# Masks at the end of a score step, another order of the attention's steps, and earlier first weights

## The chip, the core and the metric

The kernel runs on one core of a Trainium2 chip. The metric is the device time of the kernel in microseconds (us). The engines are named as in the profile: PE (matrix engine, with PEld for its weight loads), DVE (VectorE), ACT (ScalarE), POOL (GpSimd) and SP (SyncE, which here issues most DMAs).

## The reference

Three layers follow each other: attention with a block-causal mask, a mixture of experts with noisy top-2 gating, and a second one with top-1 gating and a bias per modality.

```python
# 4 batches, 8 heads, 576 positions, 64 per head; blocks of 64
scores = scale * np.matmul(q, k.transpose(0, 1, 3, 2))
mask = block_i >= block_j
scores = np.where(mask, scores, -1000000000.0)
attn = np.exp(scores - np.max(scores, axis=-1, keepdims=True))
attn = attn / (np.sum(attn, axis=-1, keepdims=True) + 1e-09)
x = np.matmul(attn, v)                       # -> 2304 rows of 512
# first layer: 8 experts, the best 2 of each row by noisy logits
noisy_logits = x @ w_gate + np.log1p(np.exp(x @ w_noise)) * noise
out[mask] += top2_w[mask, k, None] * (np.maximum(x[mask] @ w1[e], 0.0) @ w2[e])
# second layer: 8 experts, the best 1
logits = x @ w_gate + modality_bias[modality_id]
out[mask] = gate_w[mask, None] * (np.maximum(x[mask] @ w1[e], 0.0) @ w2[e])
```

## The kernel before

The kernel works in float32 accuracy by splitting values into a high part (type fp32r) and a low part, the remainder, and multiplying in three passes: high x high, high x low, low x high.

The attention goes by 16 pairs of heads (4 batches x 4 pairs), in the first 325 us of the profile. Each pair is cut into some sixty named steps. TQ, TK and T4 transpose the loaded q, k and the tail of both on PE; QH, KH, A4 (ACT) and QL, KL, D4 (DVE) make the high and low parts. S4, S6, S0 and S8 are the score steps: S4 is block row 2 (384 columns), S6 block row 3 (512 columns), S0 the rows 0 and 1 together (256 columns each), S8 the tail of 64 rows of both heads. In S4, S6 and S0 the two heads of the pair sit in the two halves of PE's rows. A score step writes two of three banks ("ps" in the profile). M steps (DVE, "nm") take maxima, E steps (ACT, "p") exponentials with sums. The B steps and BT transpose the exponentials on PE into three banks that TQ, TK, T4 and the X steps use as well ("pt"); H (ACT, "PTh") and L (DVE, "PTl") copy them out in high and low parts. VX, V0 and V1 (PE, "pa", one bank) multiply by v, CX, C0, C1 (ACT, "oT") copy that out, X0 and X1 (PE, "pt<-IW,oT") turn it back and multiply by the gates, XC0 and XC1 (ACT, "xu") copy that out, and R and R2 make the reciprocals of the sums.

The mask is added by PE as a further product in each score step: two bfloat16 matmuls per block row (one per head) add a large negative number to the 64 columns that must not count. Before, they stand behind the first of the three passes.

The order on PE, ACT and DVE is the order in which the program is written, and a small planner writes it: it keeps a clock per engine from functions of cost (`pe_cost`, `act_cost`, `dve_cost`), and among the steps whose operands are there it takes, within 0.15 us of the earliest, the one with the smallest due time. The due time of step n of pair p is p x 13.5 (the first number of `SCHED`) plus the offset of n in the table `SCHED`. POOL and SP get their order from the framework. Two other kinds of work are put between: work at fixed planner times (`at`: constants, zero fills, the first weights), and the routing of the first layer (`route`, on DVE above all, with a few matmuls), which starts when pairs 7, 11 and 15 are done and runs beside the following pairs.

`consts2` and `consts3` load and prepare what the second gate needs; `consts3` has four transposes of "wg" and one small matmul of "bias" on PE and copies on ACT. The first weights of the first expert come in four pieces of 512 KB ("xs<-in_moe_w_dram"); for each, `stage.fetch` issues the DMA and `stage.split` makes the high part on ACT ("wh<-xs") and the low part on DVE in two instructions ("wl<-xs"). They are called in the loop over NQ = 4 at planner times 110, 124, ... (fetch) and 11 later (split).

After the last pair the expert stage follows: for each expert 128-row tiles of gathered rows, two matrix products with the split weights, scatter-adds of the result. There PE works almost without a break.

Of the kernel before, what the change touches and what calls it, by code (L numbers as in the profile page):

```python
# [7 lines left out]
F32 = mybir.dt.float32  # L8
F32R = mybir.dt.float32r
BF16 = mybir.dt.bfloat16  # L10
# [5 lines left out]
DRAM = bass.MemoryType.DRAM  # L16
ET = mybir.EngineType

SCHED = (13.500, {
# [6 lines left out]
})  # L26


def moe_kernel(tc, q, k, v, w_gate, w_noise, noise, w1, w2, mod_id, w_gate2, mod_bias, m2w1, m2w2, out):
# [27 lines left out]
    clk = {"pe": 0.0, "dve": 0.0, "act": 0.0, "pool": 0.0, "base": 0.0}  # L57
# [14 lines left out]
    def cols_of(t):  # L72
        n = 1
        for x in t.shape[1:]:
            n *= x
        return n
# [7 lines left out]
    def pe_cost(name, o, i, kw):  # L84
        n = cols_of(o)
        dt = i.dtype
        if name == "transpose":
            return n * .00084
        if i.shape[0] == 64:
            return n * .00021 + .04  # L90
        return 2 * max(cols_of(i) * .00084, n * .00084) if dt == F32 else n * .000417 + .0145 * (clk["base"] is None)

    def act_cost(name, o, i, kw):
# [6 lines left out]

    gps = Timed(nc.gpsimd, "pool", pool_cost)
    vec, ten, act = Timed(nc.vector, "dve", dve_cost), Timed(nc.tensor, "pe", pe_cost), Timed(nc.scalar, "act", act_cost)

    with ExitStack() as top:
        cst = top.enter_context(tc.tile_pool(name="cst", bufs=1))
        dram = top.enter_context(tc.tile_pool(name="dram", bufs=1, space=DRAM))
        X1 = dram.tile([NT + CAP, DM], F32, name="X1")
# [37 lines left out]
        base = cst.tile([128, E], F32, name="base")  # L145
# [232 lines left out]
        def at(t, f):  # L378
            heapq.heappush(heap, (t, len(seen), f))
            seen.append(0)  # L380
# [264 lines left out]
        stage = Stage([j00, j10] + firsts + seconds)  # L645
# [144 lines left out]
        with ExitStack() as ph:  # L790
# [14 lines left out]
            masks = [cst.tile([128, n], BF16, name="mask%d" % n) for n in (128, 64)]  # L805
# [12 lines left out]
            def consts0():  # L818
                vec.tensor_scalar(IW[:, :, 0:D], bc(jp[:, None, 0:D], [128, H, D]), -64.0, None, op0=OP.is_equal)
                vec.tensor_tensor(IW[:, :, 0:D], IW[:, :, 0:D], bc(ident[:, None, 0:D], [128, H, D]), op=OP.add)  # L820
                for a in range(2):
                    for i, w in enumerate((w_gate, w_noise)):
                        nc.sync.dma_start(IW[64 * a:64 * a + 64, :, D + E * i:D + E * i + E], w.rearrange("(h d) e -> d h e", d=D))
                for t in RR:
                    nc.gpsimd.memset(t[64:128, :, 4:5], 0.0)
                for t in XU:
                    nc.gpsimd.memset(t[64:128, :, 4], 0.0)
# [32 lines left out]
            def pair(p):  # L860
# [3 lines left out]
                st = {}  # L864
# [3 lines left out]
                f = {}  # L868
# [23 lines left out]
                def khi(src, s0, n):  # L892
                    act.activation(st["kh"][:, s0:s0 + n], src, AF.Copy)

                def klo(src, s0, n):
                    vec.tensor_sub(st["kl"][:, s0:s0 + n], src, st["kh"][:, s0:s0 + n].bitcast(F32))
# [16 lines left out]
                def D4():  # L913
                    for x in halves:
# [4 lines left out]
                         TK=TK, KH=lambda: khi(st["tk"], 0, 512), KL=lambda: klo(st["tk"], 0, 512), T4=T4, A4=A4, D4=D4)  # L919
# [8 lines left out]
                def mx(o, i):  # L928
                    vec.reduce_max(nm(i), o, axis=AX, negate=True)

                def ex(o, c, i, j):
                    act.activation(P[i][:, c:c + o.shape[-1]], o, AF.Exp, bias=nm(i), scale=1.0, accum_out=st["ss"][:, j:j + 1])

                def some(name, js):

                    def tile_of(h, n):
                        return st["s", js[0], h][:, 0 if n == js[0] else 256:][:, 0:128 * (n + 1)]

                    def S_():
                        for h in range(2):  # L940
                            st["s", js[0], h] = ps_s.tile([128, 512], F32, name="ps")
                        for n in js:
                            kn = max(256, 128 * (n + 1))
                            for m, (Q, K) in enumerate(((qh, "kh"), (qh, "kl"), (ql, "kh"))):
                                for h in range(2):
                                    d = slice(64 * h, 64 * h + 64)
                                    o = st["s", js[0], h][:, 0 if n == js[0] else 256:][:, 0:kn]
                                    ten.matmul(o, Q[d, 128 * n:128 * n + 128], st[K][d, 0:kn], start=(m == 0), stop=(m == 2))
                                if m == 0:

                                    for h in range(2):
                                        d = slice(64 * h, 64 * h + 64)
                                        ten.matmul(tile_of(h, n)[:, 128 * n + 64:], masks[0][d], masks[1][d], start=False, stop=False)
                    f["S" + name] = S_
                    for h in range(2):
                        f["M%s%s" % (name, "ab"[h])] = lambda h=h: [mx(tile_of(h, n), 2 * n + h) for n in js]
                        f["E%s%s" % (name, "ab"[h])] = lambda h=h: [ex(tile_of(h, n), 0, 2 * n + h, 2 * n + h) for n in js]
# [50 lines left out]
                for h in range(2):  # L1008
# [7 lines left out]
                       lambda T, o=o, m=m: T[:, :, o:o + m + 1:m].rearrange("p h c s -> p c h s")) for i, (o, m) in enumerate(((0, 9), (16, 5)))])  # L1016

                def BT():
# [7 lines left out]
                         LT=lambda: vec.tensor_sub(end[64:128], bt(slice(64, 128)), end[64:128].bitcast(F32)))  # L1026
# [180 lines left out]

            TT, OFF = SCHED[0], dict(SCHED[1])
            OFF.update(N8=OFF["M8"] + .1, R2=OFF.pop("R"))
# [80 lines left out]
            def earliest(e, p, n):  # L1290
                t = clk[e] if p > 2 or n not in arrive else max(clk[e], arrive[n] + 5.5 * p)
                for d, k in before[n]:
                    if p >= k:
                        if (p - k, d) not in fin:
                            return None
                        t = max(t, fin[p - k, d] + (0 if d[0] in "FG" else lag[engine(d)]))
                if n[0] in bank and e == "pe":
                    b = bank[n[0]][0]
                    m = 2 if n[0] == "S" else 1
                    for r in held[b][-nbank[b]:][:max(0, len(held[b][-nbank[b]:]) + m - nbank[b])]:  # L1300
                        if r not in fin:
                            return None
                        t = max(t, fin[r] + .1)
                return t
# [5 lines left out]
            emit(0, "VS", 0)  # L1310
            emit(1, "VS", 0)
            consts0()
            for t, f in ((14, consts1), (90, consts2), (110, consts3)):
                at(t, f)
            fills = [(X1, NTT, 2), (X1, NTT + 2, 3)] + [(X2, t, 2) for t in range(0, NTT + NP + 1, 2)]
            for i, a in enumerate(fills):
                at(60 + 10 * i, lambda a=a: blank(*a))
            for i in range(NQ):
                at(110 + 14 * i, lambda: stage.fetch(1))
                at(110 + 14 * i + 11, lambda: stage.split(vec))  # L1320
            while any(todo.values()) or len(aside) > 1 or "early" not in flags:
                best = None
                for e, l in todo.items():
                    c = []
                    for i, (due, p, n) in enumerate(l[:60]):
                        t = earliest(e, p, n)
                        if t is not None:
                            c.append((t, due, i))
                    if c:
                        m = min(c)[0]  # L1330
                        t, _, i = min((x for x in c if x[0] <= m + eps), key=lambda x: x[1])
# [6 lines left out]
                if aside:  # L1338
                    t = max(aside[0][0], clk["dve"])
                    if best is None or t <= best[0] and (t <= dve_next or t > aside[0][0] + patience):  # L1340
                        best = (t, None, 0)
                t, e, i = best
# [3 lines left out]
                if e:  # L1346
                    _, p, n = todo[e].pop(i)
# [6 lines left out]
                else:  # L1354
                    clk["base"] = t
                    d = next(aside[0][1], None)
# [204 lines left out]
        with tc.For_i(0, nc.values_load(more[0:1, 0:1], min_val=0, max_val=1), 1), tc.tile_pool(name="r1", bufs=1) as r1:  # L1561
# [12 lines left out]
            with tc.For_i(0, nc.values_load(eo[0:1, NG2:], min_val=0, max_val=NG2), 1):  # L1574
# [3 lines left out]
                for i in range(B):  # L1578
                    n = slice(10 * i, 10 * i + 10)
# [20 lines left out]
                h = [hs[f][0].bitcast(F32) for f in range(NF // 128)]  # L1600
# [30 lines left out]
            with tc.For_i(0, nc.values_load(er[0:1, NG2:], min_val=0, max_val=NG2), 1):  # L1631
# [4 lines left out]
                st = Stage([j])  # L1636
# [39 lines left out]
```

## Time and profile before

| | |
|---|---|
| time, median of 3 runs | 1050.25 us (1050.09 to 1053.12) |
| profiled execution | 1052.9 us, its span 1051.1 us |
| PE busy in the span | 983.4 us (94%) |
| DVE, ACT, POOL busy | 719.2 (68%), 514.1 (49%), 491.0 us (47%) |
| mean granted clock of PE | 0.963 |
| q, k, v, weights and rows moved | 141.61 MB, 135 GB/s in the mean |

The profile is that of one execution. Busy time is time in which an engine has an instruction running; for PE the ends are modelled, so the distance from the start of one row to the start of the next says more than the length of a row. The granted clock is 1.00 at 2.4 GHz and 0.5 at 1.2 GHz; a mean between them tells which share of a stretch was spent at the lower level.

### The profile page before, as it was taken

How to read it: one execution, taken by the hardware profiler on the slowest of the kernel's cores; microseconds unless marked ns; L12 is line 12 of the kernel's file. 1: busy time of each engine (PE TensorE's matmuls, PEld its weight loads, DVE VectorE, ACT ScalarE, POOL GpSimd, SP SyncE). 2: the span in 40 equal slices, each digit the busy share in tenths (PEclk: the TensorE clock that was granted, in tenths of full speed). 3: DMA queues.
4: the chain of work that ended last, by engine and by line, in shares of the span. 5: the costliest groups of instructions: out<-in, count | busy, mean ns of one | idle time of the engine just before them, and what ended most of it. 6: DMA issues, size and time to landing. Idle time of an engine off the chain costs nothing.

```text
span 1051.1 us, 17766 instructions
## 1 busy us (share of the span) xinstructions
PE 983.4 (94%) x6186; PEld 862.2 (82%) x6186; DVE 719.2 (68%) x1761; ACT 514.1 (49%) x1172; POOL 491.0 (47%) x395
## 2 busy tenths in 40 slices
PE   7999987798879998999999999999999999999996
PEld 5778776577669887898989989898988888999995
DVE  4776657887855867866849394957798885554551
ACT  4778765666655423443333333333324454555651
POOL 4132231222311167886858484856658335342231
PEclk6999987999989999999999999999999999999998
DMA  5467433331115574665537363744267767676620
GB/s 121 104 200 219 131 79 83 75 77 46 54 42 154 160 181 110 153 165 128 119 104 139 99 142 86 148 110 89 27 162 183 257 215 252 210 223 220 209 101 12
DMA packets 158258, 141.61 MB, mean 135 GB/s; under 512 B 76233, under 2 KB 124745, under 8 KB 158034
## 3 DMA queue, kind: packets, MB, share of 16 engines
q1 hardware_dynamic: 140098, 107.18, 34.3%
q0 software_dynamic: 18064, 33.23, 15.8%
q8 instruction: 51, 0.84, 0.3%
q14 instruction: 45, 0.37, 0.1%
HBM read 112.54 MB, written 28.36 MB: 134 GB/s over the span
## 4 chain that ended last, share of the span: by engine, by line
PE 74%; DVE 11%; issue 5%; ACT 3%; POOL 2%; DMA 2%; SPq 1%; POOLq 0%; ACTq 0%
PE ph L69 28%; PE py L69 26%; PE pt L69 8%; PE ps L69 6%; PE pa L69 4%; PE px L69 2%; DVE PTl L69 2%; DVE wl L69 2%; DVE nm L69 2%; DMA xr<-X,ids 1%; ACT p L69 1%; DVE sl_ov L69 1%; POOL wl L69 1%; DVE kp L69 1%; ACT wh L69 1%
## 5 line engine op out<-in xcount | busy, mean ns | idle before, releaser
L69 POOL TENSOR_TENSOR wl<-raw,wh 128x1024 fp32r<-128x1024 f32 x80 | 207.5, 2624 | 105.3 <-ACT wh L69 91.2
L69 PE MATMUL ph<-xth,wh 128*128 128x320 f32 (+2 forms) x800 | 240.9, 301 | 2.2 <-DVE kp L69 2.1
L69 PE MATMUL ph<-xth,wl 128*128 128x320 f32 (+2 forms) x800 | 239.7, 300 | 0.0
L69 PE MATMUL ph<-xtl,wh 128*128 128x320 f32 (+2 forms) x800 | 239.6, 300 | 0.0
L69 DVE SCALAR_TENSOR_TENSOR zero<-py,gts,wgb 128x512 f32<-128x512 f32 x296 | 221.5, 748 | 8.2
L69 PE MATMUL py<-wh,kp 128*128 128x512 f32 x496 | 168.1, 399 | 3.9 <-DVE zero L69 3.9
L69 PEld LDWEIGHTS ph<-xth,wh 128*128 128x128 f32 x800 | 151.6, 189 | 4.0 <-DVE kp L69 2.8
L69 PEld LDWEIGHTS ph<-xtl,wh 128*128 128x128 f32 x800 | 151.6, 189 | 0.7
L69 PEld LDWEIGHTS ph<-xth,wl 128*128 128x128 f32 x800 | 151.6, 189 | 0.0
L69 ACT ACTIVATE wh<-raw 128x1024 fp32r<-128x1024 f32 x144 | 150.8, 1053 | 0.9 <-DMA raw<-in_moe_w_dram 0.8
L69 PEld LDWEIGHTS py<-wh,kp 128*128 128x128 f32 x496 | 94.0, 189 | 22.8 <-DVE zero L69 4.1
L69 ACT ACTIVATE yr<-py,gts 128x512 f32<-128x512 f32 x60 | 41.4, 689 | 143.6 <-PE py L69 99.8
L69 ACT ACTIVATE p<-ps,nm 128x512 f32<-128x512 f32 (+4 forms) x160 | 82.3, 522 | 36.9 <-DVE nm L69 35.4
L69 DVE TENSOR_TENSOR wl<-raw,wh 128x1024 fp32r<-128x1024 f32 x64 | 79.7, 1254 | 29.7 <-ACT wh L69 29.4
L69 DVE TENSOR_REDUCE nm<-ps 128x1 f32<-128x512 f32 (+4 forms) x160 | 69.9, 477 | 43.5 <-PE ps L69 43.2
L69 PE MATMUL py<-wl,kp 128*128 128x512 f32 x248 | 97.5, 393 | 0.0
L69 DVE SCALAR_TENSOR_TENSOR hl<-ph,hh 128x320 fp32r<-128x320 f32 (+2 forms) x100 | 46.4, 465 | 74.6 <-ACT hh L69 74.5
L69 PE MATMUL py<-wh,hh 128*128 128x512 f32 x232 | 93.8, 404 | 0.0
L69 POOL DMA_INDIRECT xr<-X,ids x55 | 57.7, 1049 | 75.1 <-PE px L69 45.0
L69 DVE TENSOR_TENSOR xtl<-px,xth 128x512 fp32r<-128x512 f32 x58 | 40.0, 690 | 77.0 <-ACT xth L69 70.9
L69 PE MATMUL py<-wh,hl 128*128 128x512 f32 x232 | 90.8, 391 | 0.0
L69 PE MATMUL py<-wl,hh 128*128 128x512 f32 x232 | 90.4, 390 | 0.0
(256 smaller groups left out, 1806.6 us busy)
## 6 DMA issues: line engine op xcount, KB each, us to landing
raw<-in_moe_w_dram SPq DMA_DIRECT2D x144, 512.0 KB
X<-zero SPq DMA_DIRECT2D x13, 512.0 KB
kld<-in_k_dram SPq DMA_DIRECT2D x32, 128.0 KB
qld<-in_q_dram SPq DMA_DIRECT2D x32, 128.0 KB
vld<-in_v_dram SPq DMA_DIRECT2D x32, 128.0 KB
X<-x SPq DMA_DIRECT2D x16, 256.0 KB
xs<-in_moe_w_dram SPq DMA_DIRECT2D x4, 512.0 KB
wgb<-WG2T POOLq DMA_DIRECT2D x1, 2048.0 KB
```

What stands on the lines that cost most here:

```text
L69: return f(*a, **kw)
```

## The change

Four things change.

1. The masks of a score step are written in one run behind all three passes of all its block rows, instead of behind the first pass of each.
2. The table `SCHED` has other offsets and a period of 13.8.
3. `pe_cost`, which only the planner reads, has other numbers for the attention: 0.1 us more where the kind of operand changes, less for each 64-row matmul, 0.02 for bfloat16.
4. `consts2` and `consts3` are put at planner times 40 and 56 instead of 90 and 110, and the fetches and splits of the first weights begin at 56 instead of 110.

```diff
-SCHED = (13.500, {
-    "T4": -21.0, "TK": -20.42, "A4": -19.22, "KH": -20.20, "D4": -18.74, "TQ": -19.70, "KL": -19.54, "QH": -19.28,
...
+SCHED = (13.800, {
+    "TQ": -13.70, "QL": -11.84, "KL": -10.99, "TK": -10.79, "QH": -9.70, "M4a": -8.45, "M4b": -7.33, "KH": -6.88,
...
-        if i.shape[0] == 64:
-            return n * .00021 + .04
+        if clk["base"] is not None:
+
+            kind = "t" if name == "transpose" or dt == F32 else dt if i.shape[0] == 64 and o.shape[-1] != 80 else "f"
+            c = {"t": .109, BF16: .02, "f": n * .000417 + .013}.get(kind, n * .00021 + .006)
+            c += .1 if kind != clk.get("kind") else 0
+            clk["kind"] = kind
+            return c
...
-                                    ten.matmul(o, Q[d, 128 * n:128 * n + 128], st[K][d, 0:kn], start=(m == 0), stop=(m == 2))
-                                if m == 0:
-
-                                    for h in range(2):
-                                        d = slice(64 * h, 64 * h + 64)
-                                        ten.matmul(tile_of(h, n)[:, 128 * n + 64:], masks[0][d], masks[1][d], start=False, stop=False)
+                                    ten.matmul(o, Q[d, 128 * n:128 * n + 128], st[K][d, 0:kn], start=(m == 0 and n == js[0]), stop=False, skip_group_check=True)
+
+                        for n in js:
+                            for h in range(2):
+                                d = slice(64 * h, 64 * h + 64)
+                                ten.matmul(tile_of(h, n)[:, 128 * n + 64:], masks[0][d], masks[1][d], start=False, stop=(n == js[-1]), skip_group_check=True)
...
-            for t, f in ((14, consts1), (90, consts2), (110, consts3)):
+            for t, f in ((14, consts1), (40, consts2), (56, consts3)):
                 at(t, f)
...
             for i in range(NQ):
-                at(110 + 14 * i, lambda: stage.fetch(1))
-                at(110 + 14 * i + 11, lambda: stage.split(vec))
+                at(56 + 14 * i, lambda: stage.fetch(1))
+                at(56 + 14 * i + 11, lambda: stage.split(vec))
```

On PE, the first S4 step before ("ps" is the score bank, "kp_157" the high and "kp_159" the low part of q):

```order
L69 MATMUL ps<-kh,kp_157 128x384 x2
L69 LDWEIGHTS mask_161
L69 MATMUL ps<-mask_162,mask_161 128x64
L69 LDWEIGHTS mask_161
L69 MATMUL ps<-mask_162,mask_161 128x64
L69 MATMUL ps<-kl,kp_157 128x384 x2
L69 MATMUL ps<-kh,kp_159 128x384 x2
```

and the same step after:

```order
L70 MATMUL ps<-kh,kp_157 128x384 x2
L70 MATMUL ps<-kl,kp_157 128x384 x2
L70 MATMUL ps<-kh,kp_159 128x384 x2
L70 LDWEIGHTS mask_161
L70 MATMUL ps<-mask_162,mask_161 128x64
L70 LDWEIGHTS mask_161
L70 MATMUL ps<-mask_162,mask_161 128x64
```

The two mask products have moved behind the third pass; their number is the same.

On DVE, the first split of weights before, which stands in pair 7 among the low halves of P and the tail of pair 8 ("kp" and "kl" there):

```order
L69 RECIPROCAL rr_165<-ss 64x1 x2
L69 TENSOR_TENSOR wl<-xs,wh 128x512 x2
L69 TENSOR_TENSOR PTl<-pt,PTh 128x384
L69 TENSOR_TENSOR PTl<-pt,PTh 128x128
L69 SCALAR_TENSOR_TENSOR kp_159<-pt,kp_157 64x64 x2
L69 TENSOR_TENSOR kl<-pt,kh 128x64
```

and after, where it stands in pair 4 ("nm" are the maxima, of S6 ahead of it and of S0 behind the tail):

```order
L70 TENSOR_REDUCE nm<-ps 128x1 x2
L70 TENSOR_TENSOR wl<-xs,wh 128x512 x2
L70 SCALAR_TENSOR_TENSOR kp_159<-pt,kp_157 64x64 x2
L70 TENSOR_TENSOR kl<-pt,kh 128x64
L70 TENSOR_REDUCE nm<-ps 128x1 x2
L70 SCALAR_TENSOR_TENSOR kp_160<-pt,kp_158 128x512
```

The other three splits follow in pairs 5, 6 and 7 at nearly the same place; before, they came in pairs 8 to 11, between steps of the routing.

On PE, the transposes of pair 9 before ("p_184", "p_182", ... are the exponentials of its block rows; the 288-wide rows are S8, first that of pair 9):

```order
L69 MATMUL ps<-kh,kp_160 128x288
L69 MATMUL pt<-ident,p_184 128x128
L69 MATMUL pt<-ident,p_182 128x128
L69 MATMUL pt<-ident,p_180 128x128
L69 MATMUL pt<-ident,p_178 128x128
L69 MATMUL pt<-ident,p_185 128x128
L69 MATMUL pt<-ident,p_183 128x128
L69 MATMUL pt<-ident,p_181 128x128
L69 MATMUL pt<-ident,p_179 128x128
```

and after:

```order
L70 MATMUL ps<-kh,kp_160 128x288
L70 MATMUL pt<-ident,p_184 128x128
L70 MATMUL pt<-ident,p_182 128x128
L70 MATMUL pt<-ident,p_180 128x128
L70 MATMUL pt<-ident,p_184 128x128
L70 MATMUL pt<-IW,oT 128x80 x4
L70 MATMUL pt<-IW,oT 64x80
```

Before, B0, B1, B2 and B3 follow each other behind S8; after, B0 stands ahead of S8, B2 behind it, and X0 and X1 of pair 8 come before B1.

## Rows read from the trace of the kernel before

**Rows 1.** Stages: stretch, its length, each engine's busy time, clock, DMA share, GB/s.

```profile
core 0: us, PE busy (x) PEld busy (x) DVE busy (x) ACT busy (x) POOL busy (x), PEclk, DMA share, GB/s
45.50:108.00 62.50, 58.84 (x461) 48.71 (x461) 44.23 (x119) 50.63 (x170) 18.11 (x26) 1.00 0.65 196
92.40:108.00 15.60, 14.67 (x116) 12.11 (x116) 10.96 (x30) 12.58 (x43) 4.42 (x6) 1.00 0.69 214
108.00:171.50 63.50, 54.00 (x360) 43.72 (x360) 41.27 (x101) 42.42 (x136) 15.53 (x21) 0.83 0.35 93
171.50:296.00 124.50, 106.16 (x741) 85.26 (x740) 105.02 (x293) 80.05 (x258) 34.67 (x41) 0.91 0.24 63
325.00:1051.00 726.00, 700.50 (x4238) 632.44 (x4236) 490.79 (x1153) 299.03 (x479) 402.73 (x243) 0.99 0.56 150
```

**Rows 2.** Waits of PE, 45 to 120 us: waiter, releaser, total, times, longest.

```profile
PE pt L69 <- PE pt L69: 3.7, 4, 0.9
```

**Rows 3.** Timeline of PE, one pair at full clock: start, length, [idle before].

```profile
92.41 0.63 PE L69 MATMUL pt<-ident,kld 128*128 128x128 f32 x4 [0.92 <-PE pt L69]
...
96.18 0.38 PE L69 MATMUL ps<-kh,kp 64*128 64x256 f32 x2
96.41 0.20 PE L69 MATMUL ps<-mask,mask 64*128 64x64 bf16 x2
96.44 0.36 PE L69 MATMUL ps<-kl,kp 64*128 64x256 f32 x2
96.64 0.40 PE L69 MATMUL ps<-kh,kp 64*128 64x256 f32 x4
96.88 0.20 PE L69 MATMUL ps<-mask,mask 64*128 64x64 bf16 x2
96.92 0.36 PE L69 MATMUL ps<-kl,kp 64*128 64x256 f32 x2
97.12 0.28 PE L69 MATMUL ps<-kh,kp 64*128 64x256 f32 x2
97.33 0.94 PE L69 MATMUL pa<-PTh,vs 128*128 128x448 f32 x4
...
107.98 0.63 PE L69 MATMUL pt<-ident,kld 128*128 128x128 f32 x4 [0.92 <-PE pt L69]
```

**Rows 4.** Waits of PE, 120 to 325 us, the two longest kinds.

```profile
PE pt L69 <- DVE PTl L69: 9.0, 10, 2.1
PE pt L69 <- DVE kl L69: 5.6, 4, 3.0
```

**Rows 5.** Timeline of PE, the S4 step of the same stretch.

```profile
104.75 0.44 PE L69 MATMUL ps<-kh,kp 64*128 64x384 f32 x2
105.03 0.20 PE L69 MATMUL ps<-mask,mask 64*128 64x64 bf16 x2
105.07 0.42 PE L69 MATMUL ps<-kl,kp 64*128 64x384 f32 x2
105.33 0.34 PE L69 MATMUL ps<-kh,kp 64*128 64x384 f32 x2
105.60 1.47 PE L69 MATMUL pt<-ident,p 128*128 128x128 f32 x10
```

**Rows 6.** Instructions on the tile xs: count, duration least/median/most in ns.

```profile
L69 DVE TENSOR_TENSOR wl<-xs,wh x8: 684/798/1747, 138.7 to 196.1; 128x512 fp32r<-128x512 f32 x8
...
L69 ACT ACTIVATE wh<-xs x4: 1051/1056/1066, 137.6 to 194.4; 128x1024 fp32r<-128x1024 f32 x4
```

**Rows 7.** Timeline of PE, 122 to 162 us, the rows with a wait.

```profile
124.40 0.39 PE L69 MATMUL pt<-bias,one 1*128 1x16 f32 x2 [1.33 <-ACT xs L69]
...
139.17 0.66 PE L69 MATMUL pt<-ident,p 128*128 128x128 f32 x4 [1.46 <-ACT xu L69]
...
141.84 1.09 PE L69 MATMUL pt<-ident,qld 128*128 128x128 f32 x4 [2.02 <-issue]
...
160.51 0.98 PE L69 MATMUL pt<-ident,p 128*128 128x128 f32 x4 [2.99 <-DVE kl L69]
```

11 rows, old and new, of the table SCHED are left out of this document.

## The prediction

> **What bounds the kernel now.** I read the windows by stage first. From 45.5 to 108 us the tensor engine is busy 58.84 of 62.5 us at full granted clock (1.00, the level of 2.4 GHz); in one pair of heads, 92.4 to 108 us, it is busy 14.67 us, ScalarE 12.58 and VectorE only 10.96 of 15.6. From 108 to 171.5 the granted clock falls to 0.83, and from 171.5 to 296 VectorE is the fullest engine after PE with 105.02 of 124.5 us (84%), because the routing steps run on it beside the attention. After 325 us PE is busy 700.50 of 726 us [rows 1]. So the attention (the first 325 us) is the part with slack, and what is saved in it moves the rest earlier one for one, as PE in the expert stage hardly waits.
>
> Then the waits of PE. Between 45 and 120 us there is one kind that repeats, four times 0.9 us [rows 2]; the timeline shows it ahead of the K transposes at 92.41 and 107.98 us, one pair, 15.57 us, apart [rows 3]. Between 120 and 325 us PE waits for VectorE: 9.0 us in ten waits for the low halves of P (PTl) and 5.6 us in four for kl [rows 4]. DMA does not appear in these lists.
>
> **The change part by part.** *Masks.* The profile shows the price of a mask between two passes. In the 256-wide step (S0) the rows start at 96.18 (kh), 96.41 (mask), 96.44 (kl), 96.64 (two kh pairs), 96.88 (mask), 96.92, 97.12, and the next work at 97.33 [rows 3]. Two kh pairs in a row take 0.24, so 0.12 each; a kl pair behind a mask takes 0.20, that is 0.08 more, and the mask itself 0.04. The step takes 1.15 us. With all masks last it is the head 0.23, five pairs of 0.12, a mask pair of 0.04, and a last mask pair with the hand-over to the next kind of work, 0.04 + (0.21 - 0.12) = 0.13: 1.00, so 0.15 less. The 384-wide step takes 0.85 [rows 5]; its kl pair takes 0.26, and 0.09 less without a mask ahead, the ending kh pair loses its own hand-over (0.27 to about 0.17): 0.28 + 0.17 + 0.17 + 0.13 = 0.75, 0.10 less. The 512-wide step has the same form; I take 0.10 too. Sum 0.35 us of PE per pair. In the nine pairs up to 171.5 us PE sets the pace, so it counts in full, in the seven after that half: 9 x 0.35 + 7 x 0.18 = **4.4 us**. Bounds: 0, if the 0.08 belongs to every kl-to-kh change, and 16 x (0.35 + 3 x 0.09) = 9.9, if the hand-over costs nothing.
>
> A rule of the Trainium skill speaks against this term. The row at 96.64 shows two pairs of the same row halves in 0.24 us: the weight load of the second hides behind the first [rows 3]. The Trainium skill, "TensorE: Matmul & The Clock Gate", in Part 3, The mechanism, says that a weight load overlaps matmuls in flight only where its row group differs. By that rule each pass pays its load wherever the masks stand, the masks' place would be worth nothing, and the sum would be 10.7. The row disagrees with it for the pairs that follow each other directly; I keep it as a rival.
>
> *Order of the steps.* In the pairs at full clock the one wait of 0.92 us per pair [rows 3] is for a transpose bank. The new order spreads the bank users differently (the last bank of the fourth-column transposes, B4, now stands ahead of S4), but ScalarE, at 12.58 us per pair [rows 1], fills a period of 14 to 15 us nearly, and the X steps now wait for its copies. I expect most of the wait to stay in another place: 0.1 us less per pair, 8 pairs, **0.8 us**; bounds 7.4 less (8 x 0.92) and 4 more (a wait of 1.4).
>
> *First weights and constants.* Each of the four splits is one ScalarE pass of 1.06 us and two VectorE passes of 0.80 us (median; one took 1.75) [rows 6]. Before, the first stands ahead of PE waits of 1.46 and 2.02 us, the second ahead of one of 2.99 [rows 7]: 6.5 us. The last two fall into the VectorE-bound stage, priced at their VectorE time, 4 x 0.80 = 3.2. In all 9.7. After, they stand in pairs 4 to 7, one per pair, each on VectorE between the maxima of S6 and those of S0, on ScalarE behind E6a, C0 or QH. Queued behind VectorE's passes are the maxima of S0 and, through E0, the transposes B0 of the same pair; behind the first two of ScalarE's the copy C0, for which V1 waits. A pair has 15.6 - 10.96 = 4.6 us of idle VectorE and 3.0 of idle ScalarE [rows 1], which hides most of it; I take 1.2 us each, 4.8, net **4.9 us** less. Bounds: hidden altogether (9.7 less) and 3.5 us each as the dearer of the two before (4.3 more). The routing constants with their 1.33 us wait [rows 7] move from about pair 8 to about pair 4 and cost there what they did: 0. Their DMAs and the weights' (four of 512 KB) go onto SP's queue among the loads and zero fills of 60 to 108 us, where the DMA share is already 0.65 to 0.69 [rows 1]; PE waits for no load there, and loads are issued three pairs ahead, so they keep cover of two periods.
>
> *Clock.* 0.83 over 63.5 us means 2 x 0.17 x 63.5 = 21.6 us at the lower level of 1.2 GHz [rows 1], in the stretch that holds the waits of 1.33 to 2.99 us [rows 7]. Half of the PE work in it, at most 9 us (21.6 / 2 x 54.00 / 63.50), is lost to that. With two splits gone from there some of these stretches should not come: **3 us** of it; bounds 0 and 9.
>
> *The stage with routing.* Before, from pair 8 on, the steps have lost the steady pattern: four sets of transposes stand in a row, each held by the copies of ScalarE and VectorE behind it. After, they alternate with S8 and X. VectorE's 105.02 us of work stay (3.2 go with the splits, counted); of its 19.5 idle us [rows 1] I let a tenth come back: **2 us**. Bounds: 10 less (half of the idle) and 5.6 more, if the waits for kl [rows 4] double.
>
> Sum: 4.4 + 0.8 + 4.9 + 3 + 2 = 15.1 us. The profiled execution took 1052.9 us (span 1051.1 and 1.8 around it), so it would take 1037.8; the median of the three runs, 1050.25, lies 2.65 below the profiled execution, and on that footing the forecast is 1035.
>
> **The rivals.**
> 1. *The moved splits break the cadence: slower.* The pairs 4 to 7 run in lock step with one wait; a block of 1.06 us on ScalarE and 1.6 on VectorE in each can push maxima, exponentials and transposes in turn. For it speaks that the second split alone stood ahead of a wait of 2.99 us; against it the 4.6 and 3.0 us of slack per pair. If a split costs 4.5 us there and the clock falls to the lower level for 13 us (6.5 us): 18 + 6.5 against 4.4 + 0.8 + 2 + 9.7 = 16.9, 7.6 us slower, 1058 us. It decides from (16.9 - 0) / 4 = 4.2 us per split, or from 2.6 with that fall of the clock.
> 2. *The gain is waited out.* From 171.5 us VectorE at 84% sets the pace; what PE saves before is given back if the routing, with the same VectorE work, still starts only when its two batches are complete, and splits cost in pairs 4 to 7 what they cost later. Then only the masks in nine pairs (3.2) and the 0.8 remain: 4 less, 1046 us. For it: VectorE's work is the same; against it: 6.5 us of waits stand ahead of this stage.
> 3. *The masks' place is worth nothing*, because each pass pays for its weights anyway: 15.1 - 4.4 = 10.7 less, 1039.5 us. Against it the 0.24 us of the two pairs [rows 3].
> 4. *All clears.* The clock stays at its upper level (8 instead of 3), a third of VectorE's idle time comes back (7 instead of 2), half the 0.92 wait goes in 8 pairs (3.7 instead of 0.8): 15.1 + 5 + 5 + 2.9 = 28, 1022 us. For it: the new order keeps one pattern through all pairs; against it: the routing cannot be planned to the tenth of a us.
>
> **How the numbers follow.** Forecast 0.45, rival 1 0.12, rival 2 0.20, rival 3 0.10, rival 4 0.13. About 0.3% (3.2 us: 1047.1 to 1053.4) is what a measurement here can tell from no change. Forecast, 3 and 4 are faster; of rival 2, at 1046 with its own spread, 0.12 is faster and 0.08 the same; rival 1 is slower. So faster 0.80, same 0.08, slower 0.12. The range leaves out rival 1 and the lower half of rival 4, 0.19 in all: 1023 to 1049.
>
> **What would show it.** In the trace of the changed kernel the mask rows stand last in a step and S0 takes about 1.0, S4 0.75 us. The K transposes come every 15.0 to 15.2 us between 60 and 110 us apart from the split pairs, which are longer by about 1; a split pair longer by 3 or more is rival 1. The granted clock from 108 to 171.5 us is above 0.9, and the last C1 copies come some 12 to 15 us earlier than 325. If S0 still takes 1.15, rival 3 is right; if the transposes at 171.5 us stand earlier but the attention still ends near 320, rival 2. The forecast is wrong altogether if PE waits for DMA in the first 110 us, or if the expert stage, 726 us now, grows.

## The result: 28 us faster, just past the quick end of the range

The changed kernel takes 1021.92 us (median of four runs, 1018.02 to 1023.02) against 1050.27 us: a ratio of 0.9717 [0.9687, 0.9748]. The sign was as forecast; the size was not: 1035 was forecast, and the range began at 1023. The profiled execution is the quickest of the four (1018.0 us, span 1016.2), so the two profiles lie 34.9 us apart and the medians 28.35: what is read from the two profiles below is more than the change gives in the median.

The windows by stage of the changed kernel answer to [rows 1]:

```profile
core 0: us, PE busy (x) PEld busy (x) DVE busy (x) ACT busy (x) POOL busy (x), PEclk, DMA share, GB/s
45.50:108.00 62.50, 60.12 (x468) 50.22 (x468) 46.21 (x123) 52.60 (x175) 19.26 (x29) 1.00 0.74 211
108.00:171.50 63.50, 58.49 (x445) 48.85 (x444) 50.36 (x135) 49.82 (x163) 17.92 (x25) 0.97 0.41 110
171.50:296.00 124.50, 110.59 (x842) 94.10 (x842) 103.01 (x290) 84.36 (x278) 35.66 (x42) 0.96 0.24 64
325.00:1016.00 691.00, 668.85 (x4054) 604.38 (x4054) 463.95 (x1084) 281.28 (x447) 397.31 (x238) 1.00 0.56 148
```

The granted clock from 108 to 171.5 us is 0.97 where it was 0.83, and 0.96 where it was 0.91 in the stage with the routing. The attention ends so early that the expert stage begins before 325. A mark in the program is better than a fixed time: the last accumulating product of each pair's second head (V1, rows "pa<-PTe"). From it in the last pair to the end of the span it is 730.1 us before and 728.6 after: nearly all that was gained lies in the attention. The distance from one pair's mark to the next:

| pairs | 1-2 | 2-3 | 3-4 | 4-5 | 5-6 | 6-7 | 7-8 | 8-9 | 9-10 | 10-11 | 11-12 | 12-13 | 13-14 | 14-15 |
|---|---|---|---|---|---|---|---|---|---|---|---|---|---|---|
| before | 15.6 | 15.6 | 15.6 | 15.6 | 17.7 | 20.7 | 24.9 | 18.4 | 25.7 | 18.5 | 19.4 | 17.2 | 23.7 | 21.2 |
| after | 15.1 | 17.2 | 15.4 | 15.0 | 15.1 | 16.9 | 15.2 | 18.5 | 19.3 | 21.8 | 16.7 | 17.0 | 19.5 | 15.6 |

Pairs are counted from 0. The steady pair is half a us shorter, and the big differences lie where the first splits stood (6-7 and 7-8: 13.5 us), in the stage with the routing, and in the last pair (5.6). The marks don't cut off quite the same work each time: after, the step 6-7 holds ten of the X matmuls that the step 7-8 lacks (30 and 10 matmuls "pt<-IW,oT", where the two steps ahead of them hold 20 each), so these two are better read together.

The two score steps of a steady pair on PE, as in [rows 3] and [rows 5] before (start, length):

```profile
103.54 0.45 PE L70 MATMUL ps<-kh,kp 64*128 64x384 f32 x2
103.82 0.34 PE L70 MATMUL ps<-kl,kp 64*128 64x384 f32 x2
104.00 0.34 PE L70 MATMUL ps<-kh,kp 64*128 64x384 f32 x2
104.18 0.20 PE L70 MATMUL ps<-mask,mask 64*128 64x64 bf16 x2
104.31 0.33 PE L70 MATMUL pt<-ident,p 128*128 128x128 f32 x1
...
110.14 0.39 PE L70 MATMUL ps<-kh,kp 64*128 64x256 f32 x2
110.37 0.29 PE L70 MATMUL ps<-kl,kp 64*128 64x256 f32 x2
110.48 0.41 PE L70 MATMUL ps<-kh,kp 64*128 64x256 f32 x4
110.71 0.30 PE L70 MATMUL ps<-kl,kp 64*128 64x256 f32 x2
110.83 0.30 PE L70 MATMUL ps<-kh,kp 64*128 64x256 f32 x2
110.94 0.26 PE L70 MATMUL ps<-mask,mask 64*128 64x64 bf16 x4
111.13 0.94 PE L70 MATMUL pa<-PTh,vs 128*128 128x448 f32 x4
```

S4 takes 0.77 us (forecast 0.75), S0 0.99 (forecast 1.00): the local price of a mask was read rightly. The 512-wide step S6 becomes 0.07 shorter (1.02 to 0.95, forecast 0.10). Pairs of passes follow each other in 0.11 to 0.12 us. The Trainium skill ("TensorE: Matmul & The Clock Gate", Part 3, The mechanism) lets a weight load overlap matmuls in flight only where its row group differs; by that, as the prediction reads it, S0 could not have become shorter, and the trace disagrees (0.99 instead of 1.15 us).

The waits of PE, 45 to 120 us (first two rows) and 120 to 325 us, answer to [rows 2] and [rows 4]:

```profile
PE pt L70 <- ACT xs L70: 0.7, 1, 0.7
PE pt L70 <- DVE kl L70: 0.6, 2, 0.4
...
PE pt L70 <- DVE kl L70: 5.8, 5, 2.1
PE pt L70 <- ACT p L70: 3.9, 4, 2.8
PE pt L70 <- DVE PTl L70: 3.4, 6, 1.2
```

The repeated 0.9 us wait is gone entirely, and waits for PTl fell from 9.0 to 3.4. Those for kl are as long as before (5.8 and 5.6).

Now the sum over the stretch from the mark of pair 1 to that of pair 15, first before, then after:

```profile
51.40:321.00 269.60, 235.08 (x1656) 192.43 (x1656) 196.81 (x531) 182.04 (x592) 72.41 (x94) 0.91 0.35 99
```

```profile
49.30:287.60 238.30, 217.00 (x1650) 181.48 (x1649) 193.31 (x531) 179.18 (x593) 71.02 (x94) 0.97 0.41 112
```

The same work takes 31.3 us less. All waits of PE listed in these two stretches add up to 34.2 us before and 20.4 after: 13.8 of it. The other 17.5 us lie in time in which PE was busy. Its clock was at the lower level for 51.2 us before, in nine stretches, and for 13.6 after, in four, 37.6 less. The first three stretches before, and the four after:

```profile
126.50:129.90 3.40, 3.40 (x19) 2.88 (x19) 0.63 (x2) 2.48 (x6) 0.00 (x0) 0.50 0.49 154
140.20:147.00 6.80, 5.16 (x24) 5.13 (x25) 5.20 (x14) 2.33 (x7) 1.19 (x2) 0.50 0.57 160
160.60:174.30 13.70, 12.01 (x51) 8.85 (x52) 11.63 (x29) 7.36 (x22) 0.25 (x1) 0.50 0.23 66
```

```profile
166.30:169.70 3.40, 3.40 (x18) 2.99 (x17) 2.15 (x9) 1.97 (x9) 1.03 (x1) 0.50 0.08 18
200.40:203.80 3.40, 3.30 (x14) 3.04 (x15) 3.40 (x6) 0.91 (x3) 0.87 (x1) 0.51 0.20 44
227.80:231.20 3.40, 3.40 (x17) 2.49 (x16) 3.31 (x8) 2.37 (x8) 0.00 (x0) 0.51 0.00 0
261.90:265.30 3.40, 3.40 (x17) 2.64 (x18) 3.37 (x6) 0.94 (x3) 0.88 (x2) 0.50 0.00 0
```

Work that runs at half speed for 37.6 us loses up to 18.8; PE was busy in 46 of the 51.2 us and in nearly all of the 13.6, which makes it at most about 16. So a good part of the gain, up to half in these two executions, is clock and not waiting. The Trainium skill ("TensorE: Matmul & The Clock Gate", Terms) has the same rule of thumb: the penalty is about the throttled time times the missing share of pulses, an estimate of 18.8 here. The trace agrees roughly: 17.5, the shorter steps included.

For the medians the granted clocks of all runs give an estimate. Four runs of the changed kernel have a mean clock of 0.979, and 49 runs of the kernel before, on four chips, one of 0.968. That is 43 and 67 us at the lower level, 24 less, which is at most 12 of the 28 us.

### The profile page after: what moved, and what is told of

Same layout as the page of the kernel before. It is cut to its first block, busy times and chain, and to the rows that moved or that the text cites. A ratio compares the mean times of both kernels' runs of the same rounds, so it can differ in the third digit from the quotient of the medians.

```text
span 1016.2 us, 17752 instructions
## 1 busy us (share of the span) xinstructions
PE 963.7 (95%) x6186; PEld 850.5 (84%) x6186; DVE 715.7 (70%) x1761; ACT 510.6 (50%) x1172; POOL 489.5 (48%) x395
## 4 chain that ended last, share of the span: by engine, by line
PE 69%; DVE 15%; ACT 5%; issue 5%; POOL 2%; DMA 2%; SPq 1%; POOLq 0%; ACTq 0%; DVEq 0%
PE ph L70 29%; PE py L70 26%; PE pt L70 7%; PE ps L70 4%; DVE PTl L70 3%; DVE nm L70 2%; PE px L70 2%; ACT p L70 2%; DVE wl L70 2%; PE pa L70 2%; DMA xr<-X,ids 1%; DVE kp L70 1%; POOL wl L70 1%; ACT wh L70 1%; DVE kl L70 1%
## 5 line engine op out<-in xcount | busy, mean ns | idle before, releaser
L70 ACT ACTIVATE yr<-py,gts 128x512 f32<-128x512 f32 x60 | 41.4, 689 | 144.1 <-PE py L70 97.9
L70 PEld LDWEIGHTS py<-wh,kp 128*128 128x128 f32 x496 | 93.2, 188 | 21.8 <-DVE zero L70 3.3
L70 ACT ACTIVATE p<-ps,nm 128x384 f32<-128x384 f32 (+4 forms) x160 | 82.9, 524 | 31.7 <-DVE nm L70 26.0
L70 ACT ACTIVATE hh<-ph 128x320 fp32r<-128x320 f32 (+2 forms) x100 | 41.9, 419 | 94.8 <-PE ph L70 86.9
```

The lines of the kernel that those rows point to most:

```text
L70: return f(*a, **kw)
```

## The experiments

Ratios are to the kernel before, run on the same chip, with their 95% intervals; "us less" is (1 - ratio) x 1050. "Steady pair" is the distance of marks between pairs 1 and 5 (where the constants or a split lengthen some of these steps, that of the others). The parts of the diff shown above are called masks (the order of the three passes and the mask products), table (`SCHED`), costs (`pe_cost`) and early (constants and first weights).

**One part alone.** Masks alone:

```diff
 kernel before
-                                if m == 0: ... masks behind the first pass
+                        for n in js: ... masks behind all passes
```

> The kernel before with one change: the masks of a score step in one run at its end; the order of all other instructions on PE, ACT and DVE stays as before. Theory A (the forecast's term): 0.35 us of PE per pair, in full where PE sets the pace: about 4.4 us faster, 1046. Rival (each pass pays for its weights wherever the masks stand): 0, 1050. If more than 8 us come, the masks were the part that I sized too low.

Measured: 0.9982 [0.996, 1.0004], 1.9 us less with 4.2 and -0.4 as ends. The steady pair went from 15.58 to 15.32, 0.26 less where the three steps would give 0.31, but the whole time hardly moved.

Early alone:

```diff
-            for t, f in ((14, consts1), (90, consts2), (110, consts3)):
+            for t, f in ((14, consts1), (40, consts2), (56, consts3)):
...
-                at(110 + 14 * i, lambda: stage.fetch(1))
-                at(110 + 14 * i + 11, lambda: stage.split(vec))
+                at(56 + 14 * i, lambda: stage.fetch(1))
+                at(56 + 14 * i + 11, lambda: stage.split(vec))
```

> The kernel before with one change: constants and first weights at the earlier planner times (40, 56, 56 on); table, costs and masks as before. Forecast's term: 4.9 us faster, 1045. Theory W (what the trace of after suggests: a split costs next to nothing in pairs 4 to 7, and each PE wait that goes from pairs 8 to 11 takes a stretch of the lower clock with it): 8 to 12 us faster, 1038 to 1042. Rival (the gain of after lies in the order alone): within 2 us of before.

Measured: 0.994 [0.9918, 0.9963], 6.3 us less (3.9 to 8.6): the forecast's 4.9 is inside, and most of theory W's range is not. The profiled run, 1039.15 us, is one of the quicker of five. From the mark of pair 1 to that of pair 15 it shows:

```profile
48.55:304.77 256.22, 222.73 (x1657) 184.03 (x1656) 194.65 (x531) 181.89 (x592) 69.50 (x94) 0.96 0.37 104
```

The waits of PE in this stretch add up to 33.2 us, hardly less than the 34.2 before. What fell is the time at the lower clock, 20.5 us instead of 51.2. One moved split is dear here too: the step 4-5 takes 21.4 us instead of 15.6, with a PE wait of 2.77 us for a PTl that stands behind the split on DVE.

Of the 6.3 us, the weights alone (the last four lines without the first two):

> The kernel before with the fetches and splits of the first weights early, and the second gate's constants at their old times. Theory: the constants' place is worth nothing, as the prediction had it, and the weights carry the whole 6 us that both gave together: 0.994 to 0.995, about 1044 us with 1050 before. Rival: the constants are worth as much as a split with a wait, 2 to 3 us: then 0.9965 or more, 1046.5 us or more.

Measured: 0.9949 [0.9923, 0.9975], 5.4 us less. The constants' share, 0.9, is inside both intervals; but these are so wide (the difference is known to about 3.5 us either way) that the rival's 2 to 3 us are not excluded. What the traces show is that the step with the constants takes 17.2 us in the changed kernel and 17.3 in that with the late times, of which more below: their place made no difference there.

Table and costs together, masks in the middle and weights late as before:

```diff
-SCHED = (13.500, {
+SCHED = (13.800, {
...
-        if i.shape[0] == 64:
-            return n * .00021 + .04
+        if clk["base"] is not None:
...
```

> The kernel before with the new table and the new planner costs for PE; masks in the middle, constants and weights late. Forecast's terms for order, routing stage and clock: 0.8 + 2 + part of 3, so 3 to 6 us faster, 1044 to 1047. Theory W: the regular pattern through the routing pairs is worth most of the missing 13 us: 15 to 18 us faster, 1032 to 1035. Rival S (the table fits only together with the masks' place and the early weights): no gain or slower, 1050 or more.

Measured: 0.9857 [0.982, 0.9895], 15.0 us less (11.0 to 18.9), from a change of order alone: theory W came true, and the 3 to 6 us that the forecast's terms would give are excluded. In its steady pairs PE waits for nothing at all; the windows of this kernel:

```profile
45.50:108.00 62.50, 62.50 (x483) 52.74 (x482) 46.92 (x129) 52.60 (x181) 18.02 (x26) 1.00 0.69 201
```

The steady pair takes 14.75 us here, with ScalarE busy 52.60 of 62.50: that engine was not too full to let the wait go, though the prediction had argued that it was. Of the 20.1 us between the marks of pairs 1 and 15 in the two profiles, 3.3 lie in the four steady pairs, 5.7 in the last, and some 11 in those between.

The table alone (first two lines of that diff):

> The kernel before with the new table of due times alone; planner costs, masks and early work as before. Theory T (the table carries the order's gain of 15 us): 14 to 17 us faster, 1033 to 1036. Theory C (the planner's PE costs carry it, because only with them it sees when a step can start): under 5 us faster, 1045 or more.

Measured: 0.9882 [0.9847, 0.9917], 12.4 us less (8.7 to 16.1). The costs alone (the others):

> The kernel before with the new planner costs for PE alone; table, masks and early work as before. Theory T: within 3 us of before, 1047 to 1053. Theory C: 10 us faster or more, 1040 or less. If the two parts only work together, both this and the table alone are within 5 us of before.

Measured: 0.991 [0.9883, 0.9936], 9.5 us less (6.7 to 12.3). Theory T and theory C each said that one part carries nearly all; neither came true, since each part alone gives most of the gain. The sum of the two, 21.9, is more than the 15.0 of both. That each takes away partly the same waits would explain it, but is not shown.

**One part undone in the changed kernel.** Masks back behind the first pass, the planner's clock kept so that the order of steps stays the same:

```diff
+                                if m == 0:
+                                    for h in range(2): ... masks behind the first pass
```

> The changed kernel with one thing put back: the masks behind the first pass of each block row, with the planner's clock kept as in the changed kernel, so that the order of all other instructions on PE, ACT and DVE is the changed kernel's. Theory A: 0.35 us per pair, 4.4 to 5.6 us slower than the changed kernel, 1026 to 1028. Rival (weights paid anyway): equal to it, 1022.

Measured: 0.9719 [0.9694, 0.9744], almost the ratio of the changed kernel itself, 0.9717. The steady pair is 15.2 instead of 15.0; the S4 step takes 0.85 again. Theory A fell in the whole time, and the rival has its time but not its cause. The clock doesn't hide a loss: the profiled run took 1022.0 us at a mean clock of 0.979, the changed kernel 1021.6 and 1022.2 at 0.978 and 0.980.

Constants and weights back at their late times:

> The changed kernel with constants and first weights put back to the late planner times (90, 110, 110 on). If the early work is worth in the new order what it is alone in the old one (6 us): 1028. Theory W (with the routing pairs free of the splits, waits there fall below what lets the clock fall): 10 to 14 us slower than the changed kernel, 1032 to 1036, with more of the lower clock between 110 and 220 us.

Measured: 0.9795 [0.9761, 0.983]. Early is worth 8.2 us here (0.9795 - 0.9717), known to about 5 either way, so it decides neither for 6 nor for theory W's 10 and more. The steps 7-8, 8-9 and 9-10, where splits stand again, take 24.7, 20.1 and 24.4 us; the changed kernel has 15.2, 18.5 and 19.3. This kernel is also that of table and costs together with the masks put last: 6.5 us less (0.9857 - 0.9795, known to about 5.5 either way), though its steady pair takes 15.05 where that had 14.75. The place of the masks changes what the planner reckons, and the order on DVE and ACT differs between the two; so masks last may be worth something through the order, where with the order kept they are not.

Old costs:

> The changed kernel with the old planner costs for PE; table, masks and early work as changed. Theory T: within 3 us of the changed kernel, 1019 to 1025. Theory C: 10 us slower or more, 1032 or more.

Measured: 0.9764 [0.9724, 0.9804], so the new ones are worth 4.9 us here, known to about 5 either way and so not quite clear of nothing. The time lies at the edge of theory T's range and far from theory C's.

Old table:

```diff
-SCHED = (13.800, {
+SCHED = (13.500, {
...
```

> The changed kernel with the old table of due times (and its period of 13.5), all else new. Theory, the parts overlap: the new costs alone gave 0.991 and the early weights with the masks took 0.9857 to 0.9717, a factor 0.9858; the product is 0.977, about 1026 us with 1050 before. In the profile the pairs at full clock come every 15.0 to 15.4 us and lower-clock stretches between 100 and 330 us add up to 14 to 30 us. Rival, the table is what carries it: without it the time falls back to 1034 us or more (0.985), with more than 35 us at the lower clock.

Measured: 0.9979 [0.9953, 1.0005]. The rival was right, and more than that: with the old table all the other changes together are worth nothing that can be measured, though the costs alone gave 9.5 us. Early and masks, added to the new costs under the old table, cost 7.2 us (0.9979 - 0.991); under the new table they gain 14.7 (0.9857 - 0.9717). It is not the old table alone that spoils them: under it with the old costs, early alone gained 6.3. The windows of this kernel show where, first the pair with the constants and the first split, then a part of it:

```profile
64.10:88.80 24.70, 20.18 (x139) 15.79 (x138) 12.88 (x34) 16.08 (x52) 5.45 (x8) 0.86 0.70 229
69.00:75.80 6.80, 6.80 (x39) 5.64 (x38) 1.77 (x7) 3.38 (x14) 1.67 (x2) 0.50 0.55 158
```

This pair takes 24.7 us instead of the 17.2 of the changed kernel, with six waits of PE between 0.41 and 1.16 us and 6.8 us at the lower clock. It is rival 1, the broken cadence, in another kernel than the one that was forecast.

**What a block of work costs.** Two blocks of ScalarE passes that nothing needs, in the changed kernel with the late weights:

```diff
+            def block(n):
+                for _ in range(n):
+                    nc.scalar.activation(dmy, zero, AF.Copy)
+            at(74, lambda: block(3))
+            at(102, lambda: block(6))
```

> The changed kernel with constants and first weights at their old, late times, and two blocks of ScalarE passes of 128x512 that nothing needs: three in a row in one pair, six in a row about two pairs later (estimated at 0.53 us each from the 1.06 us of a 128x1024 pass: 1.6 and 3.2 us). The planner does not know of them, so the order is otherwise that of the kernel with the late weights, whose pairs took 15.0 to 15.1 us there. Theory, slack and clock: ScalarE idles about 2.5 us a pair, so the short block costs under 0.5 us and the long one 1 to 3 us, and behind the long one a stretch of lower clock of about 3.4 us follows that was not there without it, in all 1 to 4 us over the 1029 us of the kernel with the late weights. Rival 1, cadence: each block is paid with its whole length, 1.6 and 3.2, and no clock falls. Rival 2: both are hidden, pairs stay at 15.1.

Measured: 0.9858 [0.982, 0.9896], 1036.78 us against 1028.98 without the blocks, 6.6 us more by the ratios where the theory had 1 to 4. The tile's row, the PE row behind the short block, and the windows of its pair, of the wait and of what follows:

```profile
L1328 ACT ACTIVATE dmy<-zero x9: 629/629/632, 83.4 to 120.1; 128x512 f32<-128x512 f32 x9
```

```profile
85.84 0.44 PE L70 MATMUL pt<-ident,p 128*128 128x128 f32 x2 [1.59 <-ACT xu L70]
```

```profile
77.40:95.40 18.00, 16.35 (x122) 14.01 (x120) 11.38 (x32) 14.87 (x46) 4.40 (x6) 0.91 0.76 244
84.25:85.84 1.59, 0.00 (x0) 0.00 (x1) 0.28 (x3) 1.56 (x5) 0.00 (x0) 1.00 1.00 233
87.00:90.40 3.40, 3.40 (x17) 3.02 (x17) 2.77 (x6) 2.10 (x7) 0.55 (x2) 0.50 0.68 236
```

The block of 1.95 us made PE wait 1.59 us, the lower clock followed for 3.4 us, and the pair grew from 15.0 to 18.0: 1.59 of wait and 1.4 of half speed. The theory, that the idle time of ScalarE would hide the short block, fell. So did rival 2; rival 1 came nearer, but a clock did fall, and the price was one and a half times the block. The long block (3.95 us) made its pair 21.1 us, 6.1 longer, with a wait of 3.80 and 6.8 us of lower clock; the next pair, which holds the constants, took 1.6 less than without the blocks.

The same blocks with the planner told of them:

```diff
-                    nc.scalar.activation(dmy, zero, AF.Copy)
+                    act.activation(dmy, zero, AF.Copy)
```

> The same two blocks of unneeded ScalarE passes in the kernel with the late weights, but now the planner is told of their length and writes the order around them. Untold, the short block (3 passes, 1.95 us on the chip) made its pair 18.0 us instead of 15.0, with a wait of PE of 1.59 us and 3.4 us of lower clock behind it, and the long one (6 passes, 3.95 us) its pair 21.1. Theory, the planner's knowledge is what hides the moved splits: told, the pair with the short block takes 15.0 to 16.2 us without lower clock, the one with the long block 16.5 to 19. Rival, a block costs what it costs and the four splits are cheap only because VectorE takes most of each: then the short one still takes 17.5 to 18.5 us with a lower-clock stretch, the long one 20 to 22. The time of the whole is no criterion, since the order of all later pairs moves too.

Measured: 0.9848 [0.9824, 0.9871]. PE rows behind the short block, and the windows of its pair and of the waits:

```profile
85.36 0.44 PE L70 MATMUL pt<-ident,p 128*128 128x128 f32 x2 [0.83 <-ACT xu L70]
86.66 0.63 PE L70 MATMUL pt<-ident,p 128*128 128x128 f32 x4 [0.86 <-DVE PTl L70]
```

```profile
76.90:93.00 16.10, 14.39 (x117) 12.27 (x116) 10.90 (x31) 13.89 (x45) 4.40 (x6) 1.00 0.80 257
84.50:88.00 3.50, 1.81 (x16) 1.54 (x15) 2.61 (x5) 3.50 (x13) 1.67 (x2) 1.00 0.77 246
```

The pair takes 16.1 us: the planner put the S4 step ahead of the waiting transposes, the wait came in two pieces, and the clock stayed at 1.00. For the short block the theory holds (1.1 instead of 3.0 us). For the long one it does not: its pair takes 22.4 us, with a wait of 2.85 and 6.8 us of lower clock. The next pair is dearer as well (19.0 us, 15.7 with the blocks untold). It seems that telling the planner helps only where it has other work to put there; two blocks in one kernel don't prove it.

## Why the prediction was wrong, step by step

**The step that failed first is "Order of the steps", forecast at 0.8 us.** With the 2 us for the stage with routing and its part of the clock's 3 it comes to 3 to 6; measured, the order alone gives 15.0 us. Two arguments of it fell. In the steady pairs the 0.92 us wait was expected to stay in another place, because ScalarE fills the period nearly; the new order has no wait there at all, and a shorter period. And the term was counted over eight steady pairs only; the order also took some 11 us from the steps between 5 and 14, for which the sum had the 2 of the stage with routing and part of the clock's 3, and 5.7 us from the last pair, which no term of the sum held.

**"Clock" (3 us) was mis-sized.** It was read in one stretch, 108 to 171.5 us, where 21.6 us at the lower level were counted. All of the attention had 51.2 us of it behind the start, 30 of them later, and 37.6 went, worth up to 16 us in these two profiles and, by the clocks of all runs, at most 12 in the medians. The bound of 9 was read from that one stretch and is no bound. The block experiment shows one way in which waits and clock hang together: a wait of 1.59 us was followed by a stretch at the lower level that cost 1.4 more. It is no fixed factor: early alone left the sum of the waits as it was and took 30.7 us of lower clock away. Nor does each long wait bring the clock down. In the kernel before, a wait of 1.94 us stands in a stretch at the upper level:

```profile
186.02 0.66 PE L69 MATMUL pt<-ident,p 128*128 128x128 f32 x4 [1.94 <-DVE PTl L69]
```

```profile
174.50:201.50 27.00, 22.37 (x167) 17.88 (x165) 22.65 (x66) 17.74 (x53) 8.13 (x10) 1.00 0.33 82
```

The prediction priced waits and clock as separate terms with independent bounds. Which waits are followed by the lower level stays open.

**"The stage with routing" (2 us) was too small.** Between the marks of pairs 8 and 15 the changed kernel needs 128.4 us (the sum of the seven steps) against 144.1, 15.7 less, waits and clock together, and with the 5.6 of the last pair.

**"First weights and constants" (4.9 us) was right in size**: 6.3 alone, 8.2 in the new order; the constants, by the steps that hold them, at nothing. But its condition was missed: the sign hangs on the order around it, since under the old table with the new costs early and masks together lose 7.2. One reading of its rows was wrong: of the two waits that follow the first split, the 2.02 us are marked "issue", time in which PE waited for nothing that the profile shows. The waits of PE in the changed kernel that follow the splits (ScalarE's passes begin at 79.22, 94.56, 109.95 and 125.55 us), the longest of each:

```profile
85.44 0.66 PE L70 MATMUL pt<-ident,p 128*128 128x128 f32 x4 [0.39 <-DVE kl L70]
...
101.06 1.40 PE L70 MATMUL pt<-IW,oT 128*128 128x80 f32 x10 [0.22 <-DVE PTl L70]
...
115.58 0.66 PE L70 MATMUL pt<-ident,p 128*128 128x128 f32 x4 [0.22 <-DVE kl L70]
...
131.19 0.66 PE L70 MATMUL pt<-ident,p 128*128 128x128 f32 x4 [0.41 <-DVE kl L70]
```

With the shorter ones behind them (0.32, none, 0.18 and 0.18) a split costs 0.2 to 0.7 us of waiting where 1.2 was taken, and the clock stays at 1.00 around them. The 17.2 us of the step 2-3 is the constants, with a wait of 0.68.

**"Masks" (4.4 us) was right in the step and wrong in the sum.** 0.99 and 0.77 us were measured for 1.00 and 0.75, the steady pair became 0.2 to 0.3 shorter, and the whole time 1.9 less in one test (4.4 is just outside its interval) and the same in the other. Two sizes were off: S6, which had no row, gives 0.07 instead of 0.10, and the three steps' 0.31 becomes 0.26 in a pair of the kernel before. By the prediction's own sum that is 3.2 (9 x 0.26 and 7 x 0.13), inside the interval of the first test. Why nothing at all is left in the other is open.

**The rivals.** Rival 3 fell by the rows, though in the whole time the masks' place is hardly worth more than it said. Rival 2 fell: the attention ended 33 us earlier in the profile. Rival 1 fell for this kernel, and came true under the old table with the new costs and, for one split, in early alone. Rival 4 had the time, 1022, by luck, with another make-up: the wait went whole instead of half, the clock gave up to twice its 8 in the profiles and at most 12 in the medians, and the last pair was not in it. Against it stood that "the routing cannot be planned to the tenth of a us"; no run tests that, and the gain came without it.

What stays open: how the 28 us of the medians divide between waits and clock, beyond the estimate of at most 12 for the clock; which waits bring the clock down; and why the new table leaves room for the splits where the old one with the new costs does not. That the planner must know the work is shown for one block only.

## What to carry to other kernels

Price a PE wait in a dense stretch as its length plus half of the lower-clock time that follows it in the same profile, and count that time over the whole kernel before bounding what another order can give. Parts of a change of order don't add: the same early work and masks gained 15 us under one table of due times and, with the same costs, lost 7 under another, so test a move together with the order that is planned for it. A saving of a few tenths of a us inside a step is shown when the whole time moves, not when the step does.

## What was not expected of the hardware

A single wait of 1.59 us in a stretch at full clock was followed by 3.4 us at 1.2 GHz, while two waits of 0.83 and 0.86 us with 0.44 us of work between them were not, and neither was one of 1.94 us in the kernel before. And the spread of one kernel's runs goes with the clock: of 49 runs of the kernel before, the four quickest (1045.95 to 1046.32 us) have a mean granted clock of 0.975, the four slowest (1053.13 to 1054.25) one of 0.962 to 0.965.
